# A planned order for two MLP passes: the port of GpSimd and VectorE in the plan, LayerNorms moved, two ordinary units moved, evictions given a lead

## The chip, the cores and the metric

The kernel runs on one core of a Trainium2 chip. A core has five engines that work side by side, each through its own queue of instructions in a fixed order: TensorE (PE, matmuls; PEld its weight loads), VectorE (DVE), ScalarE (ACT), GpSimd (POOL) and SyncE (SP, which here only issues DMAs). An engine waits on semaphores; what stands behind a waiting instruction on the same engine waits too. The metric is the device time of one launch in microseconds (us). SBUF is the on-chip memory that all engines read and write; PSUM holds matmul results until an engine copies them out (an eviction).

## The reference

```
attn = softmax(rmsnorm(q) @ rmsnorm(k).T / 8) @ v          # 4 batches, 12 heads, 448 x 64
x    = heads side by side                                   # 4 x 448 x 768
xn   = (x - mean) / sqrt(var + 1e-6) * g_ln
x    = x + relu(xn @ w_ch1) @ w_ch2                         # 768 -> 3072 -> 768
h    = relu(x @ w_in); u, v = halves of h                   # 768 -> 2 x 512
out  = (u * (w_spatial @ norm(v) + b_spatial)) @ w_out      # 512 -> 768
```

## The kernel before

The stages follow each other: attention (0 to 302 us of the profiled run), the first MLP in two passes (302 to 1026 us), then the gated MLP (1026 us to the end). The change lies in the two passes.

**The MLP.** Each float32 operand is held as a rounded part and a rest ("hi" and "lo", fp32r), and a product is three matmuls (hi hi, hi lo, lo hi). The 3072 hidden features are cut into 24 units of 128. Of unit u and batch b, `plan_hidden` does 18 matmuls of 128x448 into a PSUM tile `ph`; ACT writes the hi part of relu, DVE the lo part (L922, tile `h`). `plan_outputs` takes two units and does 6 output tiles `pm` of 6 matmuls each, and DVE adds each into `y` (L1082, 5 PSUM banks in turn). The first pass does batches 0 and 1. In it every weight block w1_u or w2_u comes by DMA as raw doubles (tile `raw`), is made float32 by one ACT and four DVE instructions (`plan_conv`; L106 to L109, into `wcA` for w1 and `wcB` for w2), is stored for the second pass, and is split into hi by ACT and lo by POOL (`plan_split`, L251, into `ws_w`). The second pass does batches 2 and 3 with the stored weights: units 0 and 1 ordinarily, the pairs p = 1 to 10 in Strassen's way (`plan_strassen`: 7 products `ph`, 63 matmuls in place of 72; DVE adds `t`, L1028), the last pair (units 22 and 23) ordinarily. Strassen needs sums of the inputs (`plan_mix`, tiles `a` by DVE L970 and POOL L973, `mix` lo parts by DVE L980) and of the weights (POOL L262, tile `wcT`). Each p from 1 to 10 also converts two pieces of the gated MLP's weights on DVE (L106 to L109 and L167, tile `wcV`).

**LayerNorm** of batches 2 and 3, which only the second pass reads, is done during the first pass: per 128 features two POOL instructions (`plan_norm_x`, L854 and L857, tile `lnx`), two on ACT and a third on POOL (`plan_xn`, L878), 18 POOL instructions a batch.

**What sets the order.** No order is written out. Each `plan_...` function lists operations by `op(n, engine, us, fn, r, w, new)`: a due time n, a duration, keys read and written, a ring of buffers. `arrange` then simulates the engines with these durations: for each engine it takes, among the operations that could start about now, the one with the lowest n, and emits its instruction. So n and the durations fix the order in which each engine's queue is written, and the chip runs that order whatever really happens. The list of before takes an operation to last the same whatever other engines do.

Of the kernel before, what the change touches and what calls it, by code (L numbers as in the profile page):

```python
# [39 lines left out]
def attention_mlp_gated(ctx, tc, q, k, v, g_q, g_k, g_ln, w1, w2, w_in, w_sp, b_sp, w_out, out):  # L40
    nc = tc.nc
    B, H, S, D = q.shape
# [108 lines left out]
    def split_out(k, n, pl, f, to, turned=False):  # L151

        rows = to.shape[0]

# [4 lines left out]
        def c():
            t = wcs["V"][:, :f]  # L160
            return t.rearrange("p (i c) -> p c i", c=NCH) if turned else t

# [10 lines left out]
        op(n, "DVE", 0.88 * f / DM, lo, r=[f"c{k}"], w=[f"r{k}"])  # L173
        dma(n + 1, f, store, r=[f"r{k}"])
# [204 lines left out]
    def arrange(bufs, window, late=None, near=0.0):  # L379
# [548 lines left out]
    def plan_hidden(u, b, n, after=()):  # L928
# [19 lines left out]
        hi, lo = parts(o, lambda: st["p"], tile_of)  # L948
        op(n, "ACT", 0.45, hi, r=["h" + o], w=["hs" + o], new=hs)
        op(n, "DVE", 0.55, lo, r=["h" + o], w=["hs" + o])  # L950

    mix = {}

    def plan_mix(z, bs, place, temp, ring, n, step, eng, since=()):
# [9 lines left out]
        for kk in range(3):  # L964
# [27 lines left out]
            for i in (0, 2, 1, 3):  # L992
                e = done[i]
                op(m + 3, "ACT", 0.45, lambda i=i, e=e, f=hi: f(i, e), r=[f"a{k}_{e}", f"mix{z}"], w=[f"S{z}_{i}_{kk}"])
                op(m + 3, "DVE", 0.55, lambda i=i, e=e, f=lo: f(i, e), r=[f"a{k}_{e}", f"mix{z}"], w=[f"S{z}_{i}_{kk}"])

    def plan_strassen(z, bs, p, n1, n2):
# [16 lines left out]
        def save(n, k, i):  # L1014
# [298 lines left out]
    with tc.manual_schedule():  # L1313
# [284 lines left out]
        plan_mix(1, bs, (place_ab, []), temp_t, "t", 0, 5, ("DVE", "vector", 0.55))  # L1598
        for p in range(1, LAST + 1):
            u, e, n = 2 * p, 2 * p + 1, start[p]  # L1600
# [5 lines left out]
            else:  # L1606
                plan_hidden(u, 2, n)
                plan_hidden(e, 2, n + H)
                plan_outputs((u - 2, u - 1), 2, n + K)
                plan_outputs((u - 2, u - 1), 3, n + 2 * K)  # L1610
                plan_hidden(u, 3, n + 3 * K)
                plan_hidden(e, 3, n + 3 * K + H)
        stay(*(f"hs{v}_{b}" for v in (u, e) for b in bs), *(f"w2_{v}b" for v in (u, e)))
# [104 lines left out]
```

## Time and profile before

| what | us |
|---|---|
| median of 3 runs (1245.27 to 1248.95) | 1245.56 |
| the profiled execution | 1243.42 |
| its span, first to last instruction | 1241.6 |
| TensorE busy in the span | 1183.4 (95%) |
| VectorE busy | 886.0 (71%) |
| GpSimd busy | 545.9 (44%) |
| ScalarE busy | 528.1 (43%) |
| mean granted TensorE clock | 0.990 |

Matmuls are pipelined in the records: each is shown longer than the step to the next, so a stretch's own length and its count of matmuls tell more than the mean of one. Idle time of an engine costs something only where the last engine waits for it.

### The profile page before, as it was taken

How to read it: one execution, taken by the hardware profiler on the slowest of the kernel's cores; microseconds unless marked ns; L12 is line 12 of the kernel's file. 1: busy time of each engine (PE TensorE's matmuls, PEld its weight loads, DVE VectorE, ACT ScalarE, POOL GpSimd, SP SyncE). 2: the span in 40 equal slices, each digit the busy share in tenths (PEclk: the TensorE clock that was granted, in tenths of full speed). 3: DMA queues.
4: the chain of work that ended last, by engine and by line, in shares of the span. 5: the costliest groups of instructions: out<-in, count | busy, mean ns of one | idle time of the engine just before them, and what ended most of it. 6: DMA issues, size and time to landing. Idle time of an engine off the chain costs nothing. (4 is left out here: it accounts for less than half of the span.)

```text
span 1241.6 us, 17013 instructions
## 1 busy us (share of the span) xinstructions
PE 1183.4 (95%) x6358; PEld 996.0 (80%) x6358; DVE 886.0 (71%) x1423; ACT 528.1 (43%) x1032; POOL 545.9 (44%) x431
## 2 busy tenths in 40 slices
PE   7999999999699799999999799999999999999998
PEld 5555655657598799999998688888888898989888
DVE  7898888875998977777754989988898564141240
ACT  5888888985434333232321343333333122223122
POOL 5757758302927622322232987565564204040200
PEclk9999999999899999999999799999999999999999
DMA  5332222123454454554415254433343128102103
GB/s 104 83 79 49 53 75 53 39 68 132 135 170 153 140 199 157 159 180 157 164 53 161 54 160 132 153 127 119 127 157 139 40 102 292 45 1 73 40 1 90
DMA packets 90903, 137.04 MB, mean 110 GB/s; under 512 B 35716, under 2 KB 66564, under 8 KB 90564
## 3 DMA queue, kind: packets, MB, share of 16 engines
q1 hardware_dynamic: 90580, 135.72, 34.6%
q8 instruction: 50, 0.82, 0.3%
q14 instruction: 33, 0.27, 0.1%
q10 hardware_dynamic: 240, 0.23, 0.1%
HBM read 97.75 MB, written 38.17 MB: 109 GB/s over the span
## 5 line engine op out<-in xcount | busy, mean ns | idle before, releaser
L1076 PE MATMUL pm<-h,ws_w 128*128 128x448 f32 x1728 | 366.7, 369 | 33.3 <-DVE y L1082 18.9
L1076 PEld LDWEIGHTS pm<-h,ws_w 128*128 128x128 f32 x1728 | 329.2, 192 | 63.8 <-DVE y L1082 23.4
L908 PE MATMUL ph<-xn,ws_w 128*128 128x448 f32 x1278 | 265.9, 362 | 2.7 <-DVE t_10p L1028 1.2
L908 PEld LDWEIGHTS ph<-xn,ws_w 128*128 128x128 f32 x1278 | 239.2, 188 | 20.3 <-DVE t_10p L1028 1.6
L1082 DVE TENSOR_TENSOR y<-pm,y 128x448 f32<-128x448 f32 x294 | 175.5, 616 | 52.0 <-PE pm L1076 51.4
L251 POOL TENSOR_TENSOR ws_w<-wcA,ws_w 128x768 fp32r<-128x768 f32 x38 | 78.8, 2073 | 187.3 <-ACT ws_w L115 162.6
L665 ACT ACTIVATE P<-s,nmx 112x448 f32<-112x448 f32 x192 | 119.8, 635 | 24.2 <-DVE nmx L660 23.1
L660 DVE TENSOR_REDUCE nmx<-s 112x2 f32<-112x896 f32 x96 | 101.0, 1082 | 22.7 <-PE s L654 21.3
L251 POOL TENSOR_TENSOR ws_w<-wcB,ws_w 128x768 fp32r<-128x768 f32 x35 | 69.0, 1971 | 72.6 <-ACT ws_w L115 72.6
L654 PE MATMUL s<-kT,qT 64*112 64x448 f32 x384 | 85.8, 562 | 4.5 <-ACT kT L639 2.3
L919 ACT ACTIVATE h<-ph 128x448 fp32r<-128x448 f32 x56 | 30.3, 541 | 125.1 <-PE ph L908 113.4
L908 PE MATMUL ph<-mix,ws_w 128*128 128x448 f32 x360 | 76.7, 365 | 4.3 <-DVE t_9U L1028 1.5
L693 PE MATMUL t<-ident,P 112*128 112x112 f32 x672 | 75.5, 260 | 2.6 <-DVE PT L706 1.7
L714 PE MATMUL po<-PT,vr 128*64 128x448 f32 x384 | 77.5, 545 | 0.4 <-ACT lnbc L832 0.3
L908 PEld LDWEIGHTS ph<-mix,ws_w 128*128 128x128 f32 x360 | 66.7, 188 | 11.6 <-DVE t_9U L1028 1.9
L693 PEld LDWEIGHTS t<-ident,P 112*128 112x128 f32 x672 | 67.1, 141 | 6.7 <-ACT P L665 3.6
L922 DVE SCALAR_TENSOR_TENSOR h<-ph,h 128x448 fp32r<-128x448 f32 x56 | 34.7, 621 | 48.5 <-ACT h L919 48.4
L714 PEld LDWEIGHTS po<-PT,vr 128*64 128x64 f32 x384 | 25.4, 136 | 49.6 <-issue 42.4
L654 PEld LDWEIGHTS s<-kT,qT 64*112 64x112 f32 x384 | 29.7, 172 | 40.1 <-issue 13.3
L1269 PE MATMUL gp<-wout,gg 128*128 128x384 f32 x336 | 58.7, 335 | 0.0
L1269 PEld LDWEIGHTS gp<-wout,gg 128*128 128x128 f32 x336 | 58.3, 188 | 0.3 <-ACT gg L115 0.3
L1163 PE MATMUL gu<-ys,winu 128*128 128x448 f32 x288 | 58.1, 362 | 0.0
(289 smaller groups left out, 1828.0 us busy)
## 6 DMA issues: line engine op xcount, KB each, us to landing
raw<-in_moe_w_ch_dram SPq DMA_DIRECT2D x48, 768.0 KB, 6.3
w1c_dram<-wcA SPq DMA_DIRECT2D x24, 384.0 KB, 5.7
w2c_dram<-wcB SPq DMA_DIRECT2D x23, 384.0 KB, 5.6
raw<-in_moe_w_in_dram SPq DMA_DIRECT2D x12, 512.0 KB, 5.1
win_dram<-raw SPq DMA_DIRECT2D x12, 512.0 KB, 2.6
wcA<-w1c_dram SPq DMA_DIRECT2D x13, 384.0 KB, 3.4
kr<-in_k_dram SPq DMA_DIRECT2D x11, 448.0 KB, 4.3
qr<-in_q_dram SPq DMA_DIRECT2D x11, 448.0 KB, 4.6
```

Source lines behind the costliest of these rows:

```text
L251: nc.gpsimd.tensor_tensor(wsp[k][:, 1, :f], of(), f32(wsp[k][:, 0, :f]), op=ALU.subtract)
L654: nc.tensor.matmul(p[:CP, j, :S], pr["qT"][rows, c * CP : (c + 1) * CP], pr["kT"][rows], start=True, stop=True)
L660: nc.vector.tensor_reduce(t, pr["s", c][:CP, :, :S], axis=AX.X, op=ALU.max, negate=True)
L665: nc.scalar.activation(pr["P", c][:, j * S : (j + 1) * S], pr["s", c][:CP, j, :S], AF.Exp, bias=pr["m", c][:, j : j + 1], scale=1.0, accum ...
L693: nc.tensor.transpose(p[:, e, c * CP : (c + 1) * CP], pr["P", c][:, w * P : (w + 1) * P], ident[:CP, :CP])
L714: nc.tensor.matmul(pr["po"][j * D : (j + 1) * D, :S], raw["v", i][:, j, w - 4 * j if z < NCH - 1 else 3], pr["PT", w], start=(z == 0), sto ...
L908: nc.tensor.matmul(to, w[:, a, w0 + kk, :], x[:, c, k0 + kk, :], start=(first and kk == 0 and m == 0), stop=(last and kk == n - 1 and m == 2),
L922: nc.vector.scalar_tensor_tensor(hid[k][:, 1, :], of(), 0.0, f32(hid[k][:, 0, :]), op0=ALU.max, op1=ALU.subtract)
L1076: nc.tensor.matmul(st["p"], s2[:, a, m * P : (m + 1) * P], hs[:, c, :], start=(u == us[0] and e == 0), stop=(u == us[-1] and e == 2),)
L1082: nc.vector.tensor_tensor(y[b][:, m, :], st["p"], y[b][:, m, :], op=ALU.add)
L1163: nc.tensor.matmul(pu[:, :S], W["u"][:, kk, a, g * P : (g + 1) * P], ys[b0 + e][:, c, kk, :], start=(kk == 0 and m == 0), stop=(kk == NK - ...
L1269: nc.tensor.matmul(po[:, :half_n], gt[g][:, a, i * P : (i + 1) * P], W["out"][:, g, e, half * half_n : (half + 1) * half_n], start=(g == 0 ...
```

## The change

Four edits, all in lists that `arrange` reads; the instructions are the same in kind and number on every engine.

1. `arrange` knows a shared port. Operations marked `port=True` (the DVE conversions, the `a` and `mix` instructions, the gate pieces' lo parts) are lengthened while POOL is planned to be busy (`shared`: DVE goes on at `SHARE` = 0.3 of its speed), and a marked DVE operation under way is lengthened when POOL starts one. The planned times of the conversions change too (0.5, 0.5, 0.95, 1.1 to 0.535, 0.535, 0.98, 0.98 for 768 columns).
2. The LayerNorms of batches 2 and 3 get other due times: batch 2 from 8 in steps of 6 to 180 in steps of 8; batch 3 from 56 (statistics) and 76 in steps of 6 to 230 and 250 in steps of 12 (us from the start of the first pass's plan).
3. The second pass takes units 0 and 1, then units 22 and 23, then the Strassen pairs 1 to 10. The output product left for after the pass is that of pair 10.
4. In the second pass evictions get a lead: `early` lowers their n by 20 us when an engine's next operation is picked.

```diff
+        def shared(us, busy):
+            if busy <= 0:
+                return us
+            return us / SHARE if us <= SHARE * busy else busy + us - SHARE * busy
...
-                found.setdefault(eng, []).append((t, n, i))
+                found.setdefault(eng, []).append((t, n - lead.get(i, 0), i))
...
+            if i in ported:
+                us = shared(us, free.get("POOL", 0.0) - t)
+            if eng == "POOL" and held_port[0] is not None and end[held_port[0]] > t:
+                d, rest = held_port[0], end[held_port[0]] - t
+                end[d] = free["DVE"] = t + shared(rest, us)
...
+    EV, SHARE, EVB = [0], 0.3, 20
+    LN2, LN3 = (180, 8), (230, 12)
...
-        plan_ln(3, 56, "o")
+        plan_ln(3, LN3[0], "o")
-        plan_norm_x(2, 8, 6)
-        plan_xn(2, xn_c, 12, 6)
-        plan_norm_x(3, 76, 6)
-        plan_xn(3, xn_c, 80, 6)
+        plan_norm_x(2, LN2[0], LN2[1])
+        plan_xn(2, xn_c, LN2[0] + 4, LN2[1])
+        plan_norm_x(3, LN3[0] + 20, LN3[1])
+        plan_xn(3, xn_c, LN3[0] + 24, LN3[1])
...
+        EV[0] = EVB
...
-        start = {p: 3 * H + 2 * K + (5.4 + K) * (p > 1) + (5.4 + 3 * K) * max(p - 2, 0) for p in range(1, LAST + 1)}
+        start = {LAST: 3 * H + 2 * K}
+        start.update((p, start[LAST] + 4 * H + 2 * K + (p > 1) * (5.4 + K) + (5.4 + 3 * K) * max(p - 2, 0)) for p in range(1, LAST))
+        order = [0, LAST] + list(range(1, LAST))
```

**VectorE, some 13 to 35 us into the first pass.** `wcA` and `wcB` rows are conversions of weights, `h` and `y` rows are evictions (for `y`, the last number of `pm_1_2` is the output tile). Before:

```order
L1082 TENSOR_TENSOR y_1504<-pm_1_1_4005,y_1504 128x448
L106 TENSOR_SCALAR wcB<-wcB 128x768
L107 TENSOR_SCALAR wcB<-wcB 128x768
L108 SCALAR_TENSOR_TENSOR wcB<-raw_3317,wcB 128x768
L106 TENSOR_SCALAR wcA<-wcA 128x768
L107 TENSOR_SCALAR wcA<-wcA 128x768
L108 SCALAR_TENSOR_TENSOR wcA<-raw_3890,wcA 128x768
L109 SCALAR_TENSOR_TENSOR wcA<-raw_3890,wcA 128x768
L109 SCALAR_TENSOR_TENSOR wcB<-raw_3317,wcB 128x768
L1082 TENSOR_TENSOR y_1504<-pm_1_2_4014,y_1504 128x448
```

Now:

```order
L1111 TENSOR_TENSOR y_1504<-pm_1_1_3980,y_1504 128x448
L1111 TENSOR_TENSOR y_1504<-pm_1_2_3991,y_1504 128x448
L106 TENSOR_SCALAR wcB<-wcB 128x768
L107 TENSOR_SCALAR wcB<-wcB 128x768
L108 SCALAR_TENSOR_TENSOR wcB<-raw_3317,wcB 128x768
L109 SCALAR_TENSOR_TENSOR wcB<-raw_3317,wcB 128x768
L106 TENSOR_SCALAR wcA<-wcA 128x768
L107 TENSOR_SCALAR wcA<-wcA 128x768
L108 SCALAR_TENSOR_TENSOR wcA<-raw_3890,wcA 128x768
L109 SCALAR_TENSOR_TENSOR wcA<-raw_3890,wcA 128x768
L1111 TENSOR_TENSOR y_1504<-pm_1_3_4002,y_1504 128x448
```

One more eviction now stands ahead of the eight conversions, which stay together. On GpSimd the instructions of the LayerNorm of batch 2 that stood around the weight splits of this place are gone:

```order
L251 TENSOR_TENSOR ws_w_3877<-wcB,ws_w_3877 128x768
L878 TENSOR_TENSOR xn_3941<-lnx_2_3970,xn_3941 128x448
L854 TENSOR_TENSOR lnx_3_4003<-y_2385,lnbc_3283 128x448
L251 TENSOR_TENSOR ws_w_3427<-wcA,ws_w_3427 128x768
L857 TENSOR_TENSOR lnx_3_4003<-lnx_3_4003,lnbc_3283 128x448
```

Now:

```order
L252 TENSOR_TENSOR ws_w_3877<-wcB,ws_w_3877 128x768
L252 TENSOR_TENSOR ws_w_3427<-wcA,ws_w_3427 128x768
L252 TENSOR_TENSOR ws_w_3878<-wcB,ws_w_3878 128x768
L252 TENSOR_TENSOR ws_w_3876<-wcA,ws_w_3876 128x768
L252 TENSOR_TENSOR ws_w_3669<-wcB,ws_w_3669 128x768
```

The splits follow each other, and the LayerNorm of batch 2 begins 21 splits further on.

**VectorE at the start of the second pass**, from the second `h` eviction on (`a` and `mix` are the inputs' sums, `wcV` and `raw` a gate piece). Before:

```order
L922 SCALAR_TENSOR_TENSOR h_3880<-ph_3_6620,h_3880 128x448
L970 TENSOR_TENSOR a_2_22_6690<-xn_4522 128x448
L192 STREAM_TRANSPOSE wcV<-raw_3317 128x448
L980 TENSOR_TENSOR mix_1_6599<-a_0_12_6608,mix_1_6599 128x448
L980 TENSOR_TENSOR mix_1_6599<-a_1_21_6611,mix_1_6599 128x448
L970 TENSOR_TENSOR a_2_11_6707<-xn_3941 128x448
L970 TENSOR_TENSOR a_2_12_6710<-xn_3941 128x448
L922 SCALAR_TENSOR_TENSOR h_3881<-ph_3_6663,h_3881 128x448
L980 TENSOR_TENSOR mix_0_6598<-a_1_11_6639,mix_0_6598 128x448
L1082 TENSOR_TENSOR y_2385<-pm_2_0_6700,y_2385 128x448
```

Now:

```order
L951 SCALAR_TENSOR_TENSOR h_3880<-ph_3_6614,h_3880 128x448
L1009 TENSOR_TENSOR mix_1_6599<-a_0_12_6610,mix_1_6599 128x448
L951 SCALAR_TENSOR_TENSOR h_3881<-ph_3_6646,h_3881 128x448
L1111 TENSOR_TENSOR y_2385<-pm_2_0_6674,y_2385 128x448
L999 TENSOR_TENSOR a_1_21_6699<-xn_5823 128x448
L1111 TENSOR_TENSOR y_2385<-pm_2_1_6683,y_2385 128x448
L999 TENSOR_TENSOR a_1_22_6710<-xn_5823 128x448
L1111 TENSOR_TENSOR y_2385<-pm_2_2_6692,y_2385 128x448
```

Between the same two `h` evictions six instructions of sums and pieces have become one, and a sum stands between two evictions from there on.

## Rows read from the trace of the kernel before

**Rows 1.** Page, part 1: busy us, share of the span, instructions.
```profile
PE 1183.4 (95%) x6358; PEld 996.0 (80%) x6358; DVE 886.0 (71%) x1423; ACT 528.1 (43%) x1032; POOL 545.9 (44%) x431
```
**Rows 2.** Windows: stretch, length, busy us (instructions) of PE, PEld, DVE, ACT, POOL, clock, DMA.
```profile
302.47:352.01 49.54, 38.93 (x181) 34.77 (x181) 40.96 (x42) 19.07 (x29) 36.26 (x23) 0.93 0.48 151
352.01:438.90 86.89, 79.16 (x387) 72.52 (x386) 80.17 (x110) 33.16 (x48) 49.63 (x29) 0.98 0.50 163
438.90:680.10 241.20, 241.20 (x1207) 226.10 (x1206) 163.57 (x246) 67.22 (x95) 66.33 (x34) 1.00 0.44 150
680.10:738.09 57.99, 47.43 (x199) 40.78 (x198) 52.82 (x56) 24.36 (x39) 50.84 (x33) 0.88 0.42 115
738.09:968.39 230.30, 219.67 (x1082) 201.28 (x1081) 206.09 (x257) 80.39 (x128) 135.58 (x89) 1.00 0.38 131
968.39:1025.99 57.60, 57.60 (x290) 54.00 (x288) 31.94 (x54) 12.95 (x22) 6.79 (x4) 1.00 0.20 76
```
**Rows 3.** Windows, TensorE alone, one Strassen period (of eight).
```profile
823.74:852.12 28.38, 27.42 (x137) 1.00 0.37 130
```
**Rows 4.** TensorE's timeline, first pass: start, length, matmuls, idle before and releaser.
```profile
336.69 4.08 PE L1076 MATMUL pm<-h,ws_w 128*128 128x448 f32 x12 [7.65 <-DVE y L1082]
...
414.28 8.27 PE L1076 MATMUL pm<-h,ws_w 128*128 128x448 f32 x32 [4.54 <-DVE h L922]
```
**Rows 5.** VectorE's timeline, first pass: one conversion early, one later.
```profile
308.96 0.85 DVE L106 TENSOR_SCALAR wcB<-wcB 128x768 f32<-128x768 f32 x1 [1.33 <-ACT wcB L105]
...
313.11 1.80 DVE L109 SCALAR_TENSOR_TENSOR wcB<-raw,wcB 128x768 uint32<-128x768 uint32 x1
...
342.75 0.56 DVE L106 TENSOR_SCALAR wcB<-wcB 128x768 f32<-128x768 f32 x1 [1.32 <-ACT wcB L105]
...
344.94 0.96 DVE L109 SCALAR_TENSOR_TENSOR wcB<-raw,wcB 128x768 uint32<-128x768 uint32 x1
```
**Rows 6.** GpSimd's timeline in the same stretch.
```profile
304.81 1.15 POOL L854 TENSOR_TENSOR lnx<-y,lnbc 128x448 f32<-128x448 f32 x1
...
315.86 2.14 POOL L251 TENSOR_TENSOR ws_w<-wcB,ws_w 128x768 fp32r<-128x768 f32 x1
```
**Rows 7.** Groups by line, 385 to 434 us: busy, mean ns, idle before.
```profile
L109 DVE SCALAR_TENSOR_TENSOR wcA<-raw,wcA 128x768 uint32<-128x768 uint32 x3 | 4.5, 1507 | 0.1
L106 DVE TENSOR_SCALAR wcA<-wcA 128x768 f32<-128x768 f32 x3 | 4.5, 1490 | 0.0
L108 DVE SCALAR_TENSOR_TENSOR wcA<-raw,wcA 128x768 int32<-128x768 int32 x3 | 4.1, 1367 | 0.0
L107 DVE TENSOR_SCALAR wcA<-wcA 128x768 int32<-128x768 int32 x3 | 2.9, 976 | 0.0
...
L857 POOL TENSOR_TENSOR lnx<-lnx,lnbc 128x448 f32<-128x448 f32 x6 | 9.5, 1593 | 0.1
...
L251 POOL TENSOR_TENSOR ws_w<-wcA,ws_w 128x768 fp32r<-128x768 f32 x3 | 6.6, 2205 | 4.8 <-ACT ws_w L115 4.8
L251 POOL TENSOR_TENSOR ws_w<-wcB,ws_w 128x768 fp32r<-128x768 f32 x3 | 5.6, 1865 | 2.4 <-ACT ws_w L115 2.4
```
**Rows 8.** Windows, the middle of the first pass.
```profile
500.00:600.00 100.00, 100.00 (x502) 93.74 (x501) 75.20 (x113) 30.92 (x42) 27.52 (x14) 1.00 0.45 152
```
**Rows 9.** TensorE's timeline, start of the second pass.
```profile
685.30 8.04 PE L1076 MATMUL pm<-h,ws_w 128*128 128x448 f32 x25 [2.14 <-POOL ws_w L251]
699.10 4.85 PE L1076 MATMUL pm<-h,ws_w 128*128 128x448 f32 x12 [5.76 <-DVE y L1082]
```
**Rows 10.** GpSimd's timeline, start of the second pass.
```profile
676.10 2.97 POOL L973 TENSOR_TENSOR a<-a,a 128x448 f32<-128x448 f32 x2 [14.12 <-DVE a L970]
...
683.05 2.20 POOL L251 TENSOR_TENSOR ws_w<-wcX,ws_w 128x768 fp32r<-128x768 f32 x1
```
**Rows 11.** VectorE's timeline, a Strassen pair.
```profile
824.92 2.23 DVE L108 SCALAR_TENSOR_TENSOR wcV<-raw,wcV 128x512 int32<-128x512 int32 x1
```
**Rows 12.** TensorE's timeline, the same Strassen pair.
```profile
830.86 8.68 PE L1076 MATMUL pm<-h,ws_w 128*128 128x448 f32 x42 [0.96 <-DVE y L1082]
```

More of the change, by code (lines that the diff above doesn't have):

```diff
@@ L172, in split_out @@
         op(n, "ACT", 0.73 * f / DM, hi, r=[f"c{k}"], w=[f"r{k}"])
-        op(n, "DVE", 0.88 * f / DM, lo, r=[f"c{k}"], w=[f"r{k}"])
+        op(n, "DVE", 0.88 * f / DM, lo, r=[f"c{k}"], w=[f"r{k}"], port=True)
         dma(n + 1, f, store, r=[f"r{k}"])
@@ L227, in plan_conv @@
         op(n, "ACT", 0.8 * e, lambda: conv(0), r=[f"r{k}"], w=[c], new=ring or "wc" + wc)
-        for z, us in enumerate((0.5, 0.5, 0.95, 1.1), 1):
-            op(n + z, "DVE", us * e, lambda z=z: conv(z), r=[f"r{k}"], w=[c])
+        main = wring != "wraw0"
+        for z, us in enumerate((0.535, 0.535, 0.98, 0.98) if main else (0.5, 0.5, 0.95, 1.1), 1):
+            op(n + z, "DVE", us * e, lambda z=z: conv(z), r=[f"r{k}"], w=[c], port=main)
         return pl
@@ L360, in at, with op @@
         return 8 * i + AT[nm] + EARLY.get(nm, {}).get(i, 0)
-    def op(n, eng, us, fn, r=(), w=(), new=None, mode=None):
+    lead, ported = {}, set()
+    def op(n, eng, us, fn, r=(), w=(), new=None, mode=None, early=0, port=False):
+        if early:
+            lead[len(ops)] = early
+        if port:
+            ported.add(len(ops))
         ops.append((n, eng, us, fn, tuple(r), tuple(w), new, mode))
@@ L450, in arrange @@
                 rings[new].append(w[0])
+            if i in ported:
[3 more added lines that the diff above has]
+                end[d] = free["DVE"] = t + shared(rest, us)
+                for o in after[d]:
+                    if o in ready:
+                        ready[o] = max(ready[o], end[d] + late["DVE"])
             end[i] = free[eng] = t + us
+            if eng == "DVE":
+                held_port[0] = i if i in ported else None
             for d in after[i]:
@@ L459, in arrange @@
         ops.clear()
+        lead.clear()
+        ported.clear()
     ap, raw, prepared = {}, {}, {}
@@ L948, in plan_hidden @@
         hi, lo = parts(o, lambda: st["p"], tile_of)
-        op(n, "ACT", 0.45, hi, r=["h" + o], w=["hs" + o], new=hs)
-        op(n, "DVE", 0.55, lo, r=["h" + o], w=["hs" + o])
+        op(n, "ACT", 0.45, hi, r=["h" + o], w=["hs" + o], new=hs, early=0 if after else EV[0])
+        op(n, "DVE", 0.55, lo, r=["h" + o], w=["hs" + o], early=0 if after else EV[0])
     mix = {}
@@ L985, in plan_mix @@
             for e in ("21", "22", "11", "12"):
-                op(m, eng[0], eng[2], lambda e=e, f=whole: f(e), r=[f"mix{z}"], w=[f"a{k}_{e}"], new=ring)
+                op(m, eng[0], eng[2], lambda e=e, f=whole: f(e), r=[f"mix{z}"], w=[f"a{k}_{e}"], new=ring, port=True)
             done = {0: "22", 1: "11", 2: "21", 3: "12"}
@@ L994, in plan_mix @@
                 op(m + 3, "ACT", 0.45, lambda i=i, e=e, f=hi: f(i, e), r=[f"a{k}_{e}", f"mix{z}"], w=[f"S{z}_{i}_{kk}"])
-                op(m + 3, "DVE", 0.55, lambda i=i, e=e, f=lo: f(i, e), r=[f"a{k}_{e}", f"mix{z}"], w=[f"S{z}_{i}_{kk}"])
+                op(m + 3, "DVE", 0.55, lambda i=i, e=e, f=lo: f(i, e), r=[f"a{k}_{e}", f"mix{z}"], w=[f"S{z}_{i}_{kk}"], port=True)
     def plan_strassen(z, bs, p, n1, n2):
@@ L1018, in f @@
                 act_copy(st[k], st["b", i])
-            op(n, "ACT", 0.45, f, r=[f"b{i}{g}"], w=[f"t{k}{g}"], new="t")
+            op(n, "ACT", 0.45, f, r=[f"b{i}{g}"], w=[f"t{k}{g}"], new="t", early=EV[0])
         def add(n, k, i, of, into=None):
@@ L1031, in add @@
             w = [f"t{into or k}{g}"]
-            op(n, "DVE", 0.55, f, r=[f"b{i}{g}", f"t{of}{g}"], w=w, new=None if into else "t")
+            op(n, "DVE", 0.55, f, r=[f"b{i}{g}", f"t{of}{g}"], w=w, new=None if into else "t", early=EV[0])
         def finish(n, of, key, k):
             hi, lo = parts(k, lambda: st[of], lambda: following("hs", hs_of))
-            op(n, "ACT", 0.45, hi, r=[f"t{key}{g}"], w=["hs" + k], new="hs")
-            op(n, "DVE", 0.55, lo, r=[f"t{key}{g}"], w=["hs" + k])
+            op(n, "ACT", 0.45, hi, r=[f"t{key}{g}"], w=["hs" + k], new="hs", early=EV[0])
+            op(n, "DVE", 0.55, lo, r=[f"t{key}{g}"], w=["hs" + k], early=EV[0])
         def c22():
@@ L1085, in plan_outputs @@
             op(n + 0.6 * len(us) * m, "PE", 0.6 * len(us), o_pe, r=r, w=[k], new=pl)
-            op(n + 0.6 * len(us) * (m + 1), "DVE", 0.55, o_dve, r=[k], w=[f"y{b}_{m}"])
+            op(n + 0.6 * len(us) * (m + 1), "DVE", 0.55, o_dve, r=[k], w=[f"y{b}_{m}"], early=0 if pls else EV[0])
     gt = {}
@@ L1572, in temp_t @@
             return ap["t"].tile([P, S], F32, tag="t", name=name)
-        start = {p: 3 * H + 2 * K + (5.4 + K) * (p > 1) + (5.4 + 3 * K) * max(p - 2, 0) for p in range(1, LAST + 1)}
+        start = {LAST: 3 * H + 2 * K}
+        start.update((p, start[LAST] + 4 * H + 2 * K + (p > 1) * (5.4 + K) + (5.4 + 3 * K) * max(p - 2, 0)) for p in range(1, LAST))
+        order = [0, LAST] + list(range(1, LAST))
         extra = list(range(len(pieces)))
-        for p in range(LAST + 1):
+        for p in order:
             u, e = 2 * p, 2 * p + 1
             n = start.get(p, 0)
-            use = start.get(p + 1, n + 4 * K) + (12.6 if p < LAST - 1 else K) if p else 0
+            use = (start[p + 1] + 12.6 if p < LAST - 1 else n + 5.4 + 3 * K) if 0 < p < LAST else n + 4 * H if p else 0
             for z, v in enumerate((u, e)):
@@ L1598, in attention_mlp_gated @@
         plan_mix(1, bs, (place_ab, []), temp_t, "t", 0, 5, ("DVE", "vector", 0.55))
-        for p in range(1, LAST + 1):
+        for p in order[1:]:
             u, e, n = 2 * p, 2 * p + 1, start[p]
@@ L1606, in attention_mlp_gated @@
             else:
[L1607 to L1612, printed above, removed]
+                for z, (v, b) in enumerate(((u, 2), (e, 2), (u, 3), (e, 3))):
+                    plan_hidden(v, b, n + H * z)
+                plan_outputs((u, e), 2, n + 4 * H)
+                plan_outputs((u, e), 3, n + 4 * H + K)
+        u, e = 2 * LAST - 2, 2 * LAST - 1
         stay(*(f"hs{v}_{b}" for v in (u, e) for b in bs), *(f"w2_{v}b" for v in (u, e)))
@@ L1620, in attention_mlp_gated @@
         for z, b in enumerate((2, 3)):
-            plan_outputs((NU - 2, NU - 1), b, 7 * z)
+            plan_outputs((NU - 4, NU - 3), b, 7 * z)
         plan_win(l1, 1, "v", 0)
```

1 line of the change is left out of this document (added).

## The prediction, made before the changed kernel was run

> **What bounds the kernel now.** I read the page's busy shares first: TensorE is busy 95% of the span [rows 1], so at most some 58 us can be won without taking matmuls away, and the change takes none. The second view is the windows over the two MLP passes. In the middle of the first pass 1207 matmuls fill 241.20 us without a gap: 0.200 us each [rows 2]. At that rate the other stretches' matmuls leave a rest, which is the time lost there, idle or at a low clock:
>
> - A1, 302.47 to 352.01: 49.54 - 181 x 0.2 = 13.3 us
> - A2, 352.01 to 438.90: 86.89 - 379 x 0.2 - 0.8 (eight small transposes of the LayerNorm are among the 387) = 10.3
> - A3, to 680.10: 0
> - B1, 680.10 to 738.09, the second pass's start and Strassen pairs 1 and 2: 57.99 - 199 x 0.2 = 18.2
> - B2, to 968.39, eight Strassen pairs of 135 matmuls: 230.30 - 8 x 27.0 = 14.3
> - B3, to 1025.99, 288 matmuls: 0
>
> In all 56.1 us [rows 2]. The third view is TensorE's timeline with what ended each gap. It names VectorE nearly each time: 7.65 us for an eviction `y`, 4.54 for an `h` [rows 4], 5.76 for a `y` at the start of the second pass [rows 9], 0.96 in each Strassen pair [rows 12]. A gap costs more than itself: after the 7.65 us, 12 matmuls took 4.08 us where 2.4 would do, and after the 4.54 us, 32 took 8.27 in place of 6.4 [rows 4]; the granted clock over B1 is 0.88, and 1.00 over A3 [rows 2].
>
> The fourth view, VectorE beside GpSimd, shows why the evictions are late. VectorE is in order, and the conversions ahead of an eviction last as long as GpSimd makes them. With GpSimd in the LayerNorm, L106 and L109 of one weight took 0.85 and 1.80 us; with GpSimd idle, 0.56 and 0.96 [rows 5]. From 385 to 434 us, where the other LayerNorm runs, a weight's four conversions mean 1.51 + 1.49 + 1.37 + 0.98 = 5.34 us [rows 7], against 2 x 0.56 + 2 x 0.96 = 3.04 alone. GpSimd pays too: 1.59 us for a LayerNorm instruction [rows 7] that took 1.15 alone [rows 6].
>
> **The change part by part.** The sum is made against the profiled execution, 1243.42 us; the median of the runs shown is 2.1 us above it. No engine gains or loses an instruction, so everything lies in the 56.1 us. Attention and the gated MLP keep their order.
>
> *LayerNorm of batch 2 leaves A1.* Its 18 GpSimd instructions no longer meet the first conversions. The first weight, w2_1, was converted from 308.96 to 314.91 us [rows 5]; at 3.04 us it is done at 312.0, and its split, which ended 3.1 us behind it at 318.0 [rows 6], ends near 315, some 1 us after TensorE comes to it. The 7.65 us gap was a `y` behind eight conversions in VectorE's queue; one more eviction now goes ahead of them, and the eight take 2 x 3.04 us. What can be late next is a conversion that waits for the store of the block before it in `wcA` or `wcB`; by my walk along the queues there is about 1 us of room at the tightest place. I keep 1.5 of the 13.3 (bounds 0, and 7 if that room is missed once, with the low clock behind it).
>
> *LayerNorm of batch 3 leaves A2.* The `h` evictions no longer stand behind conversions of 1.4 to 1.8 us. What then runs in A2 is the pattern of A3, which lost nothing; I keep 0.5 of the 10.3 (0 to 5).
>
> *Both go into A3.* There VectorE is busy 75.2 of 100 us, or 21.7 of a 28.8 us period (two units), and GpSimd 27.5 of 100 [rows 8]. A period converts four weights; if all four meet GpSimd as from 385 to 434, they cost 4 x 2.3 = 9.2 us more, and VectorE needs 30.9 of 28.8. Batch 2 has a step of 8 us, so 10.8 of its instructions a period at 1.59, and four splits at about 2.05: GpSimd 25.4 of 28.8, so all four may well meet it. Over batch 2's 48 us this is 48 / 28.8 x 2.1 = 3.5 us lost; batch 3 with a step of 12 has 7.2 instructions a period, GpSimd 19.7, and by proportion to the stretch measured (17 LayerNorm instructions and six splits, 39 of 49 us) VectorE needs 29.5: 0.7 us a period, 1.8 in 72 us. That is some 5 if nothing is placed with care; the plan now counts the port and can put a conversion between GpSimd's instructions. I take 4, with bounds of 0 and 21.6, the whole loss of A1 and A2 carried along.
>
> The Trainium skill (SBUF — State Buffer, section "SBUF: two separate sides") says that the port pair is an exclusive lock: whichever of the two engines starts first holds it for its whole instruction and the other fully blocks. By that rule a period of batch 2's stretch holds the port for 12 us of conversions (4 x 3.04), 12.4 of LayerNorm (10.8 x 1.15) and 7.4 of splits (4 x 1.86), 31.8 of 28.8, an estimate of 5.0 us lost in 48; batch 3's stretch fits. So the sum would be 1 us higher by the rule, which also speaks against the planner's 0.3. The trace agrees in part: both engines are stretched, but by about 0.5 us an instruction and not by the other's whole length [rows 6, 7].
>
> *Start of the second pass.* The split of w2_1 for the second pass stands behind four GpSimd sums as before: from 676.10, with 1.47 each [rows 10] and no wait between them, and then 2.20 for the split, it ends at 684.1 instead of 685.25; TensorE wants it five matmuls into the outputs, at 681.1. So 3.0 us of gap stay, and 2.3 for the clock behind it (the 25 matmuls after the old gap took 8.04 less 0.17 of drain, 2.9 too many [rows 9]). The next gap, 5.76 us, and the slow matmuls behind it (12 in 4.85) were an eviction behind `a` and `mix` instructions; in the new order a sum stands between evictions, and the pairs that need the sums begin 28.8 us later. The weights of units 22 and 23 are split instead, four of about 2 us; GpSimd reaches them near 684, and the first is wanted behind 72 matmuls and the gap, at about 697.5. Evictions have five PSUM banks of 1.2 us behind them, so one conversion of 2 us in front hides. I keep 5.3 for the start (2 to 18.2).
>
> *Strassen pairs.* Each loses 1.37 (28.37 against 27.0) [rows 3], because three conversions of a gate piece, up to 2.23 us beside GpSimd's splits [rows 11], stand ahead of the last `t` and first `y`. The lead moves evictions ahead one by one; the second piece goes behind the third product's `t`. VectorE cannot leave a conversion that has begun, so a late eviction of up to 2 us remains possible. I take half, 0.7 for each of ten pairs, 7.0 (0 to 17).
>
> *End of the pass.* Pair 10 now ends it, and its last `h` have 7.2 us of outputs of their own batch ahead of them and 14.4 of pair 9 before; B3 keeps 0. The first load of the gated MLP's weights was issued long after it could have been and has 28.8 us of outputs to hide in.
>
> Sum of what stays: 1.5 + 0.5 + 4 + 5.3 + 7.0 = 18.3 of 56.1. Gain 37.8: 1243.42 - 37.8 = 1205.6 for the profiled execution, and with the 2.1 us, 1208 for the median.
>
> **The rivals.** All are times of the median.
>
> R1: the LayerNorms carry their loss along. For it: VectorE is asked for 30.9 of 28.8 us. Against it: steps of 8 and 12 in place of 6, and no conversions that start from nothing. A3 then loses 21.6 in place of 4: 1225.
>
> R2: the second pass's start meets a new wait, on the weights of units 22 and 23, which must be loaded and split before any Strassen weight. For it: GpSimd stood at 50.84 of 57.99 us in B1 [rows 2]. Against it: 13 us of room. B1's start keeps its 18.2: 1208 + 12.9 = 1221.
>
> R3: the lead does nothing in the Strassen pairs, since the conversion under way is the one that hurts and it cannot be overtaken. Ten pairs at 1.37 and the 3.3 that pairs 9 and 10 lost beyond it: 17.0 in place of 7.0, 1218.
>
> R4, slower: A3 had no gap in 241 us, so its order can only get worse, and its whole order is new, not only where the LayerNorms stand. If in each of its 8.4 periods an `h` comes as late as at 414.28, that is 4.54 of gap and 1.7 of clock, 6.2 each: 52 us in place of 4, 1256. It decides against the change from a loss of 41.8 in A3 on, 5.0 a period. Against it: outside the LayerNorms VectorE has a quarter of its time free [rows 8].
>
> **How the numbers follow.** Chances: forecast 0.50, R1 0.15, R2 0.10, R3 0.15, R4 0.10, of which 0.06 lies beyond its deciding point by more than 0.3% and 0.04 about it. 0.3% is 3.7 us, about what a measurement of this kernel tells from no change. The forecast's own range is 1199 to 1216. The range to hold 8 in 10 reaches over R3, R2 and R1, to 1230, and down to 1195, where nearly everything lost is won (1187 to 1189 would be all of it); it leaves out R4 and the ends. Faster by over 0.3%: 0.90; within: 0.04; slower: 0.06.
>
> **What would show it.** Right: windows over the first 137 us of the first pass with some 2 us over 0.200 a matmul; conversions there of 0.56 and 0.96; TensorE's gaps in the pass only in the stretch of the LayerNorms, 480 to 600 us, and there a few us; one gap of about 3 us behind a POOL split at the start of the second pass; Strassen periods near 27.7. Wrong: gaps of 4 us and a clock below 1.00 in the middle of the first pass (R1, R4), a gap for `ws_w` about 14 us into the second pass (R2), periods still at 28.4 (R3). A gap ahead of the gated MLP's first matmuls would show that the end, which I count at nothing, was wrong.

## The result, and the profile after

The changed kernel takes 1200.64 us (median of 5 runs, 1197.67 to 1201.95), the kernel before beside it 1247.27 (5 runs): ratio 0.962, 95% interval 0.960 to 0.964. The profiled execution of after took 1198.12 us in place of 1243.42. 1208 was forecast, so some 7 us more were won than the sum had.

The page's busy shares after (columns as in [rows 1]):

```profile
PE 1172.6 (98%) x6358; PEld 992.5 (83%) x6358; DVE 881.7 (74%) x1423; ACT 530.3 (44%) x1032; POOL 548.5 (46%) x431
```

The counts are those of [rows 1], and VectorE's work is 4 us less of 886: the time was won by when things happen, not by less work. The windows of after, cut between TensorE's stages: A1 and A2 in one (it ends 36 matmuls later in the work than in [rows 2]), A3, the start of the second pass up to the first Strassen product, the Strassen pairs, and the outputs of pairs 9 and 10 that end the pass (compare [rows 2]):

```profile
300.97:421.80 120.83, 119.94 (x595) 111.33 (x596) 97.59 (x136) 38.39 (x52) 34.69 (x18) 1.00 0.55 180
421.80:658.18 236.38, 235.66 (x1178) 219.48 (x1178) 194.34 (x259) 81.63 (x119) 115.44 (x70) 1.00 0.46 154
658.18:706.89 48.71, 45.76 (x217) 41.50 (x216) 41.66 (x53) 18.15 (x30) 41.83 (x28) 0.96 0.33 89
706.89:949.48 242.59, 241.49 (x1207) 226.02 (x1206) 215.44 (x277) 92.16 (x144) 154.10 (x95) 1.00 0.41 135
949.48:981.05 31.57, 29.35 (x145) 26.85 (x144) 22.17 (x38) 9.19 (x16) 3.06 (x2) 1.00 0.31 122
```

At 0.200 us a matmul (one of 596 is missing among the PE records of the first row) these lose 1.6, 1.6 (eight small transposes taken off as before), 5.3, 1.2 and 2.6 us: 12.3 in all, against 56.1 before. That makes 43.8 us; by their lengths the two passes are 43.4 us shorter, of the 45.3 between the two spans. Most of the rest is the attention stage, which ended at 300.97 instead of 302.47. Its end lay between 300.97 and 303.60 in all the traces of this study, so this part is within the scatter.

TensorE's timeline of after, the gaps that are left (start, length, matmuls, idle before and releaser):

```profile
524.25 6.68 PE L1105 MATMUL pm<-h,ws_w 128*128 128x448 f32 x32 [0.36 <-DVE h L951]
...
662.08 15.25 PE L1105 MATMUL pm<-h,ws_w 128*128 128x448 f32 x67 [2.44 <-POOL ws_w L252]
...
729.76 2.08 PE L937 MATMUL ph<-mix,ws_w 128*128 128x448 f32 x9 [1.10 <-ACT t_2p L115]
...
965.50 0.67 PE L1105 MATMUL pm<-h,ws_w 128*128 128x448 f32 x2 [0.86 <-ACT ws_w L115]
967.54 13.67 PE L1105 MATMUL pm<-h,ws_w 128*128 128x448 f32 x67 [1.37 <-POOL ws_w L252]
```

Where VectorE ended nearly all the gaps of [rows 4, 9, 12], it now ends only small ones. The two that count wait for a weight's split: one forecast (662.08), one not (965.50 and 967.54, at the end of the pass).

A Strassen period of after (compare [rows 3]):

```profile
814.48:841.48 27.00, 27.00 (x136) 1.00 0.41 137
```

27.00 where the forecast had 27.7. In the stretch of the LayerNorms (compare [rows 8]) VectorE and GpSimd have both grown and TensorE has hardly noticed:

```profile
500.00:600.00 100.00, 99.42 (x500) 92.45 (x499) 86.44 (x123) 37.13 (x54) 50.58 (x32) 1.00 0.49 160
```

VectorE beside GpSimd in after, two conversions (start, length) and then the two splits that they met:

```profile
323.12 2.50 DVE L108 SCALAR_TENSOR_TENSOR wcA<-raw,wcA 128x768 int32<-128x768 int32 x1
...
328.18 2.10 DVE L107 TENSOR_SCALAR wcB<-wcB 128x768 int32<-128x768 int32 x1
```

```profile
322.71 2.09 POOL L252 TENSOR_TENSOR ws_w<-wcB,ws_w 128x768 fp32r<-128x768 f32 x1 [4.96 <-ACT ws_w L115]
327.62 2.23 POOL L252 TENSOR_TENSOR ws_w<-wcA,ws_w 128x768 fp32r<-128x768 f32 x1 [2.82 <-issue]
```

L108 began 0.41 us into the split and ended at 325.62, 0.82 behind its end (324.80), and takes 0.96 alone. L107 ended 0.43 behind its split and takes 0.56 alone. In the two passes of after 59 conversions of 768 columns stand in rows of their own and began while a GpSimd instruction was under way. L106 and L107 ended 0.41 to 0.46 us behind it, L108 and L109 0.81 to 0.82, whether 0.1 or 1.8 us of it was left. So these conversions got next to nothing done while GpSimd worked. The evictions that read PSUM (`y`, `t`, `h` from `ph`; 243 rows, 136 of them beside GpSimd's work) took 0.55 to 0.63 throughout.

### The profile page after: what moved, and what is told of

It is laid out like the page before. It is cut to its first block, busy times and chain, and to the rows that moved or that the text cites. A ratio compares the mean times of both kernels' runs of the same rounds, so it can differ in the third digit from the quotient of the medians.

```text
span 1196.3 us, 16979 instructions
## 1 busy us (share of the span) xinstructions
PE 1172.6 (98%) x6358; PEld 992.5 (83%) x6358; DVE 881.7 (74%) x1423; ACT 530.3 (44%) x1032; POOL 548.5 (46%) x431
## 4 chain that ended last, share of the span: by engine, by line
PE 53%; DVE 8%; DMA 3%; POOL 1%; issue 1%; ACT 1%; SPq 0%; ACTq 0%; DVEq 0%; POOLq 0%
PE pm L1105 19%; PE ph L937 16%; PE gp L1298 5%; PE gu L1192 5%; PE gv L1144 5%; PE gs L1219 3%; DMA w1c_dram<-wcA 2%; DVE y L1111 2%; DMA w2c_dram<-wcB 1%; DVE wcA L109 1%; DVE wcB L108 1%; POOL a L1002 1%; DVE wcB L109 1%; DVE wcA L108 1%; DVE wcA L107 1%
## 5 line engine op out<-in xcount | busy, mean ns | idle before, releaser
L1105 PE MATMUL pm<-h,ws_w 128*128 128x448 f32 x1728 | 357.7, 364 | 6.1 <-POOL ws_w L252 4.0
L1105 PEld LDWEIGHTS pm<-h,ws_w 128*128 128x128 f32 x1728 | 323.8, 188 | 32.9 <-POOL ws_w L252 5.3
L1192 PEld LDWEIGHTS gu<-ys,winu 128*128 128x128 f32 x288 | 54.0, 187 | 3.8
```

The costliest lines, as they stand in the source:

```text
L1105: nc.tensor.matmul(st["p"], s2[:, a, m * P : (m + 1) * P], hs[:, c, :], start=(u == us[0] and e == 0), stop=(u == us[-1] and e == 2),)
L1192: nc.tensor.matmul(pu[:, :S], W["u"][:, kk, a, g * P : (g + 1) * P], ys[b0 + e][:, c, kk, :], start=(kk == 0 and m == 0), stop=(kk == NK - ...
```

## The experiments

One table for all. The first pass is counted from its first hidden-layer matmuls to the first output matmul of the second pass, the second from there to the first matmul of the gated MLP (rows of TensorE's timeline). Ratios are to the kernel before, run beside each.

| kernel | median us | ratio (95%) | first pass | second pass |
|---|---|---|---|---|
| before | 1243 to 1247 | 1 | 377.6 | 345.9 |
| after | 1200.64 | 0.962 (0.960 to 0.964) | 357.2 | 322.9 |
| e1 LayerNorms back | 1227.10 | 0.987 (0.985 to 0.988) | 383.9 | 324.4 |
| e2 port off | 1234.62 | 0.993 (0.992 to 0.995) | 369.3 | 346.3 |
| e3 no lead | 1213.18 | 0.976 (0.975 to 0.977) | 357.4 | 336.7 |
| e4 port off, old order | 1236.13 | 0.994 (0.993 to 0.996) | 369.7 | 346.2 |
| e5 costs only (share 1.0) | 1234.77 | 0.993 (0.991 to 0.994) | 368.2 | 346.2 |
| e12 share 0.6 | 1225.86 | 0.986 (0.984 to 0.987) | 366.0 | 340.7 |
| e6 share 0.05 | 1205.35 | 0.968 (0.966 to 0.970) | 362.6 | 324.4 |
| e11 pieces unmarked | 1211.65 | 0.974 (0.973 to 0.975) | 357.6 | 334.3 |
| e7 LayerNorms close | 1206.65 | 0.970 (0.968 to 0.971) | 362.2 | 322.9 |
| e8 two weights early | 1196.61 | 0.962 (0.961 to 0.964) | 357.5 | 319.8 |
| e9 after again | 1199.76 | 0.965 (0.963 to 0.966) | 357.0 | 322.9 |
| e10 last weight early | 1196.30 | 0.962 (0.961 to 0.964) | 356.9 | 320.0 |

**e1, the LayerNorms back**

```diff
-    LN2, LN3 = (180, 8), (230, 12)
+    LN2, LN3 = (8, 6), (56, 6)
```

> After with the LayerNorms' old due times (8 in steps of 6; 56 and 76 in steps of 6), all else as after; so the first pass has the port in its plan and nothing more. Theory L (the LayerNorms' move is what frees the first 137 us, the prediction's terms A1 and A2): the first pass loses most of its 20.4 us again, conversions there last 0.85 to 1.8 us as before, and the time is 1200.6 + 15 to 20 = 1216 to 1221. Rival P (the port in the plan does it, by putting conversions between GpSimd's instructions): gaps stay below 1 us and the time is within 3 of 1201.

Rival P fell, and theory L's figures with it: the first pass loses not most of its 20.4 us but 26.7, and is 6.3 us longer than before. Three rows of ScalarE, then TensorE's, at its start:

```profile
314.53 0.67 ACT L901 ACTIVATE lnx<-lnx,gl_c 128x448 f32<-128x448 f32 x1 [1.81 <-POOL lnx L886]
...
319.15 0.67 ACT L901 ACTIVATE lnx<-lnx,gl_c 128x448 f32<-128x448 f32 x1 [3.34 <-POOL lnx L886]
...
320.33 0.83 ACT L115 ACTIVATE ws_w<-wcB 128x768 fp32r<-128x768 f32 x1
```

```profile
321.21 1.11 PE L1105 MATMUL pm<-h,ws_w 128*128 128x448 f32 x2 [8.48 <-ACT ws_w L115]
```

The weight was converted at 313.51, but its split stood behind LayerNorm instructions in ScalarE's queue, one of which waited 3.34 us for GpSimd, whose LayerNorm was itself stretched by conversions. The old gap was a late eviction; this one is a late weight. The port in the plan alone makes the first pass worse.

**e2, the port off**

```diff
-        if port:
-            ported.add(len(ops))
...
-        for z, us in enumerate((0.535, 0.535, 0.98, 0.98) if main else (0.5, 0.5, 0.95, 1.1), 1):
+        for z, us in enumerate((0.5, 0.5, 0.95, 1.1), 1):
```

> After with no operation marked for the port and the conversions' old planned times; the LayerNorms moved, new order and lead kept. Theory L: the first 137 us stay near their 2 us of loss; between 480 and 620 us, where the plan no longer sees the port, the 4 us of the prediction's term for the LayerNorms in A3 come up, in place of the 0.7 seen; the Strassen pairs stay at 27.0 since the lead is there: 1203 to 1206. Rival P: the port in the plan made the conversions harmless everywhere, so gaps of 2 us and more come back in both passes, Strassen periods near 28: 1212 or more. Rival N: the port's edit is worth nothing, 1199 to 1202.

Rival P. The LayerNorms' move alone wins 8.4 of the first pass's 20.4 us, and the second pass wins nothing, though it has the new order and the lead. VectorE, then TensorE, in the stretch of the LayerNorms (TensorE's last row is of a Strassen pair):

```profile
556.92 0.98 DVE L106 TENSOR_SCALAR wcB<-wcB 128x768 f32<-128x768 f32 x1
557.94 1.41 DVE L107 TENSOR_SCALAR wcB<-wcB 128x768 int32<-128x768 int32 x1
559.39 1.80 DVE L108 SCALAR_TENSOR_TENSOR wcB<-raw,wcB 128x768 int32<-128x768 int32 x1
561.22 2.47 DVE L109 SCALAR_TENSOR_TENSOR wcB<-raw,wcB 128x768 uint32<-128x768 uint32 x1
563.62 1.14 DVE L949 SCALAR_TENSOR_TENSOR h<-ph,h 128x448 fp32r<-128x448 f32 x2
```

```profile
564.28 8.27 PE L1103 MATMUL pm<-h,ws_w 128*128 128x448 f32 x32 [2.44 <-DVE h L949]
...
819.02 8.68 PE L1103 MATMUL pm<-h,ws_w 128*128 128x448 f32 x42 [0.98 <-DVE y L1109]
```

Four conversions in a row, planned at 3.05 us, took 6.66, and the `h` behind them was late. The Strassen pairs have their 0.98 us gap before a `y` again (the last row). Together with e1, for the first pass: the LayerNorms alone give 8.4 us, the port alone -6.3, both 20.4. The worth of either edit depends on the other.

**e3, no lead**

```diff
-    EV, SHARE, EVB = [0], 0.3, 20
+    EV, SHARE, EVB = [0], 0.3, 0
```

> After with a lead of 0 in place of 20 us; all else as after. Theory E (the lead is what took the Strassen pairs' 1.37 us a pair): periods are 28.4 again, ten pairs: 1200.6 + 11 to 14 = 1212 to 1215. Rival P (the port in the plan took it: sums and pieces no longer put in front of late evictions): periods stay at 27.0 and the time at 1199 to 1203.

Rival P on the pairs, which stay at 27.0 but for two gaps of about 1 us; wrong on the total. The second pass is 13.8 us longer than after's, and 12.7 of them lie before its first Strassen product. Windows of TensorE alone, the start and then the pairs (after: 48.71 and 242.59):

```profile
659.26:720.65 61.39, 49.08 (x217) 0.86 0.32 88
720.65:964.40 243.75, 241.75 (x1207) 1.00 0.38 131
```

VectorE's and TensorE's rows at the start:

```profile
659.82 5.94 DVE L1009 TENSOR_TENSOR mix<-a,mix 128x448 fp32r<-128x448 f32 x3
...
677.97 6.27 DVE L999 TENSOR_TENSOR a<-xn 128x448 f32<-128x448 f32 x4
684.16 0.61 DVE L1111 TENSOR_TENSOR y<-pm,y 128x448 f32<-128x448 f32 x1
```

```profile
684.82 2.61 PE L1105 MATMUL pm<-h,ws_w 128*128 128x448 f32 x6 [4.01 <-DVE y L1111]
693.28 6.93 PE L1105 MATMUL pm<-h,ws_w 128*128 128x448 f32 x23 [5.85 <-DVE y L1111]
```

Four sums, 6.27 us together, stand in front of an eviction. The lead's place is here.

**e4, port off and the old order** (e2's edit, and the second pass in its old order; part of the diff)

```diff
-        for p in order:
+        for p in range(LAST + 1):
...
-            plan_outputs((NU - 4, NU - 3), b, 7 * z)
+            plan_outputs((NU - 2, NU - 1), b, 7 * z)
```

> As the kernel without the port's edit, and the second pass in its old order too (units 22 and 23 last); LayerNorms moved and lead kept. To be read against the kernel without the port's edit, run beside it, so that the order's part stands alone. Theory O (the order frees the start of the second pass, as the prediction has it: 5.76 us of gap and the slow matmuls behind it): the first 58 us of the second pass lose 12 to 18 us, against some 5 to 7 in the other kernel, so 6 to 11 us slower than it. Rival E (the lead alone frees the start, since evictions go ahead of sums in either order): within 2 us of the other kernel at the start; the end of the pass has no wait for a weight (the 2.2 us that after lost there), so it may even be 1 to 2 us faster.

346.2 against 346.3: without the port in the plan the new order is worth nothing in sum. Theory O fell for that case: the first 72 output matmuls, 14.4 us at 0.200, take 30.82 us in the old order and 29.92 in the new. The sum hides two larger parts, though: from the first Strassen product to the last the new order (e2) is 3.4 us shorter (254.42 against 257.77 for the same matmuls), and at the pass's end, where the old order loses nothing, the new order's last 144 matmuls take 33.14 us in place of 28.8. The old order with the port at 0.3 has no plan: `arrange` comes to a point where no operation can start. So what the new order is worth with the port is open.

**e5, e12, e6: the share**

```diff
-    EV, SHARE, EVB = [0], 0.3, 20
+    EV, SHARE, EVB = [0], 1.0, 20     # e12: 0.6; e6: 0.05
```

> After with SHARE 1.0 in place of 0.3: a marked operation is never lengthened in the plan, so of the port's edit only the conversions' planned times stay (0.535, 0.535, 0.98, 0.98). All else as after. Theory P (the plan gains because it knows that conversions last longer beside GpSimd and so puts evictions between them): close to the kernel without the port's edit, 38 us over after; that is 1228 to 1238, Strassen pairs with the 0.98 us gap before a y. Rival C (the corrected costs did it, or any other order would have): 1197 to 1208, no gaps in the Strassen pairs.

> After with SHARE 0.6: in the plan a marked operation keeps 0.6 of its speed while GpSimd works. With 1.0 it was 34 us over after, with 0.05 about 8. Theory B (a wide basin: any figure that lengthens the conversions clearly does most of it): 1200 to 1210. Rival V (each figure gives another order, and only near 0.3 is it good): 1215 to 1230.

> After with SHARE 0.05 in place of 0.3: in the plan a marked VectorE operation all but stops while GpSimd works. The rows of the Strassen pairs look like that: L107 beside a split took 1.97 us and ended 0.2 us behind it, 128x512. Theory S (what counts is that the plan knows of the port at all; the figure matters little): within 4 us of after, 1193 to 1201 against a before of 1243. Rival V (0.3 is a fitted value, the order it gives is a lucky one): 1205 or more, with gaps spread over both passes.

With 1.0 the time is that of e2: the corrected durations are worth nothing, the marks everything. With 0.6 the passes are 11.6 and 5.2 us shorter than before, against 9.4 and -0.3 with 1.0 and 20.4 and 23.0 with 0.3: rival V. With 0.05, between S and V, the second pass is 1.5 us longer than after's and the first 5.4, most of that in one place:

```profile
573.60 0.67 PE L1105 MATMUL pm<-h,ws_w 128*128 128x448 f32 x2 [0.76 <-ACT ws_w L115]
576.10 4.47 PE L1105 MATMUL pm<-h,ws_w 128*128 128x448 f32 x11 [1.82 <-POOL ws_w L252]
```

From 1.0 to 0.6 and to 0.3 each step helps; 0.05, which is nearer to what the rows on VectorE beside GpSimd show, is some 5 us slower by the medians. One late weight among the LayerNorms is no trend. Whether 0.3 is a good figure or only gave a lucky order stays open.

**e11, the pieces unmarked**

```diff
-        op(n, "DVE", 0.88 * f / DM, lo, r=[f"c{k}"], w=[f"r{k}"], port=True)
+        op(n, "DVE", 0.88 * f / DM, lo, r=[f"c{k}"], w=[f"r{k}"])
...
-            op(n + z, "DVE", us * e, lambda z=z: conv(z), r=[f"r{k}"], w=[c], port=main)
+            op(n + z, "DVE", us * e, lambda z=z: conv(z), r=[f"r{k}"], w=[c], port=main and kind != "gate")
```

> After with the gate pieces' instructions (conversions and lo parts of wcV, second pass) not marked for the port; weights' conversions of the first pass and the inputs' sums stay marked. Theory G (in the Strassen pairs the marks on the pieces alone decide, since three conversions in a row ahead of the last t and first y are what cost 1.4 us a pair): first pass 357, start of the second pass within 1 us of after, Strassen pairs 28.4 each: 10 to 14 us more than after, 1211 to 1215. Rival S (the sums' marks shape the pairs too, or the lead does it once the pass starts in order): pairs at 27.0, within 3 us of after.

Theory G, with 11.4 us in the second pass. VectorE in a Strassen pair of e11, with TensorE's wait:

```profile
845.47 1.65 DVE L106 TENSOR_SCALAR wcV<-wcV 128x512 f32<-128x512 f32 x1 [0.49 <-ACT wcV L105]
847.14 1.97 DVE L107 TENSOR_SCALAR wcV<-wcV 128x512 int32<-128x512 int32 x1
849.15 2.23 DVE L108 SCALAR_TENSOR_TENSOR wcV<-raw,wcV 128x512 int32<-128x512 int32 x1
851.31 0.61 DVE L1057 TENSOR_TENSOR t_6U<-ph,t_6U 128x448 f32<-128x448 f32 x1
```

```profile
855.09 5.27 PE L1105 MATMUL pm<-h,ws_w 128*128 128x448 f32 x25 [0.96 <-DVE y L1111]
```

And in after, a conversion of the pair's first piece and then the second piece, which is the one above:

```profile
832.81 1.97 DVE L107 TENSOR_SCALAR wcV<-wcV 128x512 int32<-128x512 int32 x1
...
841.22 1.58 DVE L106 TENSOR_SCALAR wcV<-wcV 128x512 f32<-128x512 f32 x1 [0.21 <-ACT wcV L105]
842.72 0.61 DVE L1057 TENSOR_TENSOR t_6U<-ph,t_6U 128x448 f32<-128x448 f32 x1
843.25 0.61 DVE L1111 TENSOR_TENSOR y<-pm,y 128x448 f32<-128x448 f32 x1
843.79 1.30 DVE L107 TENSOR_SCALAR wcV<-wcV 128x512 int32<-128x512 int32 x1
845.00 0.61 DVE L1111 TENSOR_TENSOR y<-pm,y 128x448 f32<-128x448 f32 x1
```

Conversions that meet a split are as long as ever (1.97), but evictions come between those of the second piece, where e11 has three conversions in a row. The plan with the port doesn't spare the contention, and it doesn't get its length right either: it makes an L106 or L107 of 512 columns last 0.357 / 0.3 = 1.19 us beside a split, where the rows have 1.30 to 1.97. That is long enough for an eviction to be due when the planner picks VectorE's next instruction.

**e7, the LayerNorms at a step of 6**

```diff
-    LN2, LN3 = (180, 8), (230, 12)
+    LN2, LN3 = (180, 6), (228, 6)
```

> After with the LayerNorms in the middle of the first pass at the old step of 6 us each (batch 2 from 180, batch 3 from 228 and 248), in place of 8 and 12; port and all else as after. Theory M (room: at a step of 6 GpSimd is asked for some 31 of 28.8 us a period, VectorE too, which no order can hide): 4 to 7 us more than after, gaps between 480 and 570 us. Rival P (the plan with the port takes the LayerNorms anywhere, even at 6): within 1.5 us of after.

Theory M by size: the first pass is 5.0 us longer, but in one place, not over the stretch:

```profile
575.19 0.67 PE L1105 MATMUL pm<-h,ws_w 128*128 128x448 f32 x2 [2.57 <-ACT ws_w L115]
577.85 2.60 PE L1105 MATMUL pm<-h,ws_w 128*128 128x448 f32 x6 [1.99 <-POOL ws_w L252]
```

**e8, e9, e10: two weights earlier.** In e10 the last weight gets a free buffer of the other ring (first diff); e8 also splits w2 of unit 1 for the second pass at the end of the first (second diff).

```diff
-                    plan_split(f"w2_{v}b", "w2", lambda z=z: wcs["WX"[z]], f"cw2_{v}b", use - (20, 14)[z], "wsb")
+                    tail = p == LAST - 1 and z == 1
+                    plan_split(
+                        f"w2_{v}b", "w1" if tail else "w2", lambda z=z: wcs["WX"[z]], f"cw2_{v}b",
+                        use - (20, 14)[z], "wsa" if tail else "wsb",
+                    )
```

```diff
         due["w1", 1, 1] = due["w2", 0, 1] = n
+        due["w2", 1, 1] = n + 12
...
+        keep("w2_1b", "wsb")
...
-                if v:
+                if v > 1:
```

> After with two weights split earlier: w2 of unit 1 for the second pass is loaded and split at the end of the first pass (before the inputs' sums on GpSimd), and w2 of unit 21, the last, goes into a buffer of the w1 ring, which is free once the last Strassen products are done, in place of one that pair 9's outputs hold to the last. Theory W (the 2.44 us gap with its low clock at the second pass's start, and the 0.86 and 1.37 us gaps in its last outputs, come from these two weights): both gaps go, 4.0 + 2.3 us with the clock, so 5 to 6.5 us faster than after: ratio to before 0.957 to 0.958. Rival N (behind each gap stands another: evictions at the start, the h of pair 10 at the end): 0 to 2 us.

> The changed kernel as it is, run beside the next one, so that a difference of 2 us can be told. Every theory: ratio to before 0.960 to 0.964, first pass 357.2 us long, second pass 322.9, as in its first trace.

> After with only the last weight of the second pass (w2 of unit 21) split into a buffer of the w1 ring. Theory W: the 0.86 and 1.37 us gaps before the last outputs go, with a little clock behind them; 2.2 to 2.6 us faster than the changed kernel beside it, ratio to it near 0.998. Rival N (run to run scatter of the attention stage, some 2 us between traces, is as large): the second pass is 2.3 us shorter in the trace, the two times can't be told apart.

The end of the pass in e10, one row for 144 output matmuls without a gap:

```profile
949.65 28.96 PE L1105 MATMUL pm<-h,ws_w 128*128 128x448 f32 x144
978.45 1.75 PE L1144 MATMUL gv<-winv,ys 128*128 128x512 f32 x7
```

The second pass is 2.9 us shorter than in e9, the changed kernel beside it; the medians are 3.5 apart (1196.30 and 1199.76), with intervals that still touch (0.9606 to 0.9638, 0.9631 to 0.966). So e10 is probably faster than the changed kernel, by about 3 us; the gaps are gone for certain (theory W). e8 won at the end too (its median comes from another set of runs than e9's), and at the start rival N holds: the 2.44 us gap is gone, but evictions behind `mix` instructions come late instead:

```profile
667.84 1.48 PE L1105 MATMUL pm<-h,ws_w 128*128 128x448 f32 x6 [1.51 <-DVE y L1111]
```

## Why the prediction was right, and where it wasn't

The bound and the size of what could be won were right: the whole gain lies in the 56.1 us that TensorE lost, and 12.3 stay where 18.3 were forecast. That the sum came so near is in part luck. It laid the gain on the LayerNorms' move, the new order and the lead, and gave the port's edit one clause; taken out of the finished kernel, that edit costs some 35 us (e2), most of the gain. And the terms missed both ways. By its terms:

- *A1 and A2*: 2.0 forecast, 1.6 measured; early conversions of 0.56 and 0.96 as expected. But the reason was short. I gave the LayerNorms' move both terms; e2 shows that it wins 8.4 of the pass's 20.4 us alone, e1 that the port alone loses 6.3. The 20.4 us need both.
- *The LayerNorms in A3*: 4 forecast, 1.6 for the whole of A3. The clause that decided is the one on the plan that counts the port: without it (e2) gaps of 1.41 and 2.44 us stand there, and at a step of 6 with it (e7) 5.0 us. My 30.9 us of VectorE in 28.8 had every conversion meet GpSimd; in the windows VectorE is busy 86.44 of 100 there, so the plan kept many apart.
- *The second pass's start*: 5.3 forecast, 5.3 measured, with a gap of 2.44 for the 3.0 forecast, and 67 matmuls in 15.25 us behind it. The evictions that are no longer late there are the lead's work (e3, 12.7 us) on top of the port's (e2); that the order frees them too was not shown (0.9 us in e4, without the port).
- *The Strassen pairs*: 7.0 forecast, 1.2 measured, and here the step failed. I wrote that the lead moves evictions ahead and that half of the loss would stay, since a conversion that has begun can't be left. The lead does next to nothing there (e3 without it loses 1.2 us more than after in all ten pairs, e2 with it has the old gaps), as rival R3 said; but R3's time, 1218, didn't follow, because the port's marks on the pieces break up the row of conversions (e11). I had priced the port edit in the first pass alone.
- *The end of the pass*: 0 forecast, 2.6 lost. I looked at the `h` of pair 10 and at the gated MLP's load, not at the buffers of its weights: with the ordinary pair no longer last, the second weight of pair 10 waits for a buffer that pair 9's outputs hold until just before (e10 takes the wait away).

R1, R2 and R4 did not come: A3 lost 1.6 us, no gap stands before units 22 and 23, and the clock is 1.00 in every stretch but the start of the second pass (0.96).

On the port I took the wrong side. I read means by line, 0.5 us more an instruction, as both engines going on more slowly. Single rows of both engines beside each other show that a conversion that meets a GpSimd instruction under way gets next to nothing done until its end: it ends 0.41 to 0.46 or 0.81 to 0.82 us behind it, and takes 0.56 or 0.96 alone. The Trainium skill (SBUF — State Buffer, section "SBUF: two separate sides") states that the port pair is an exclusive lock between GpSimd and some kinds of VectorE instruction, held for the whole instruction by whichever starts first. The trace agrees. The planner's 0.3 is therefore a figure that served, not a measure of the port.

## What to carry to other kernels

A planner that fixes an order should know of what its engines share: correcting durations for each engine alone won nothing here, and taking out the growth beside the other engine cost more (some 35 us) than taking out the LayerNorms' move (27) or the lead (13). In the Strassen pairs the growth helps by letting due work in between. Edits to one plan are not additive, so take each out of the finished kernel as well as putting it in alone. And when another piece of work becomes the last, look at the buffers of its weights as well as its data.

## What the runs showed of the hardware

A VectorE conversion that starts while a GpSimd instruction is running waits for that one, up to 1.8 us here, whatever its own length. An eviction from PSUM keeps its 0.61 us beside the same work, but the lo part of `h` made from a `t` tile, which lies in SBUF and takes 0.61 alone, took up to 2.33:

```profile
719.77 2.33 DVE L951 SCALAR_TENSOR_TENSOR h<-t_1U,h 128x448 fp32r<-128x448 f32 x1 [0.64 <-ACT h L948]
```

The mean of a group of instructions hides this, since it mixes those that met with those that didn't.
